# Cached grouped-query attention on one core: how the output weight and two V blocks are spread over the DMA engines, and where two groups of transposes stand

## The chip, the cores and the metric

The kernel runs on one core of a Trainium2 chip. The metric is the device time of one execution in microseconds (us), as a median of runs. A profile of one execution is at hand: its span runs from the first to the last instruction, and the execution's own time is a little longer than that.

## The reference

```python
B, Sq, D = 8, 4, 512
Hq, Hkv, Sk, Dh = 32, 8, 2048, 128          # all tensors bf16
q = (x @ wq).reshape(B, Sq, Hq, Dh).transpose(0, 2, 1, 3)
k = jnp.repeat(k_cache, 4, axis=1)           # k_cache, v_cache: (B, Hkv, Sk, Dh)
v = jnp.repeat(v_cache, 4, axis=1)
scores = jnp.einsum("bhqd,bhkd->bhqk", q, k) * (Dh ** -0.5)
p = softmax(scores, axis=-1)
o = jnp.einsum("bhqk,bhkd->bhqd", p, v)
out = o.transpose(0, 2, 1, 3).reshape(B, Sq, Hq * Dh) @ wo      # wq (512, 4096), wo (4096, 512)
```

The two caches are 32 MB each, wq and wo 4 MB each; everything else is small.

## The kernel before, in words

**Units.** The work is cut into 16 units: a batch entry and a group of four of the eight K/V heads (first all eight entries of one group, then of the other). A unit has one K block and one V block of 2 MB, each laid out as 128 partitions with 16 KB a partition. K0 is the first K block and K15 the last.

**Loads.** All big loads are issued by SP, on one queue. A list fixes their order: K0, wq, x, K1, K2, V0, then K and V in turn. `load_ready` issues what has a free buffer; there are three buffers for K and three for V, so SP waits for the transposes of a K block or the V products of a V block before it issues the load that reuses the buffer. The output weight wo, 4096 rows of 512, is read in four passes p of 1024 rows. Before, passes 0 and 1 come in two shapes: `load_wo_e` brings, in eight small loads strewn between the K and V loads, 64 partitions' worth of rows (eight partitions a load, 64 KB) into the tile `wo_e`; `load_wo_m` brings the remaining 768 rows of a pass into `wo_sb`. Passes 2 and 3 are one load each (`load_wo`). Part of pass 0 goes ahead of V14, the rest of wo after V15. Then come seven loads of 2 to 14 rows of x into the tile `spare`, which nothing reads; they are there to show in a profile when the DMA engines have got so far, and are called probe loads here.

**Step n of the main loop** (n from 1 to 17) works on three units at once. It transposes K of unit n in four parts (`transpose_part`: PE transposes into `kp`, DVE copies to `kt`), makes the scores of unit n - 1 (`scores`: PE matmuls into `s_ps`, ACT exponentials into `s_sb` with row sums), turns the probabilities of unit n - 1 so that the keys lie on partitions (`probs_to_keys`: eight PE transposes into `pt`, four ACT copies into `probs`), and for unit w = n - 2 makes the sums for the normalisation (`norms`), the products with V (`values`, in two halves of 32 matmuls into `o_ps`) and the scaled result `oT` (`finish`). The order in which PE takes these within a step is the order of the source. A manual schedule keeps it; each engine runs its own instructions in order and waits on semaphores.

**Output.** After the eight units of a head group, `to_tokens` turns `oT` to tokens and `to_wo_rows` turns it to the row layout in which wo was loaded (`oE`, `oM` for the first group, `oP` for the second). `project(p, r0, n)` adds n rows of pass p to `out_ps`, two matmuls a row. At the end ACT copies `out_ps` to `out_sb`, and two DMAs, one from ACT and one from SP, write the output.

The lines of the profile that the prediction speaks of are those of the functions above: 97 (K loads), 105 (V loads), 116, 120 and 124 (wo), 400 (probe loads), 177 and 178 (K transposes and copies), 247 and 255 (scores, exponentials), 265 and 271 (`probs_to_keys`), 304 (`values`), 356 (`project`), 409 (the copy to `out_sb`).

Of the kernel before, what the change touches and what calls it, by code (L numbers as in the profile page):

```python
# [8 lines left out]
BF16 = mybir.dt.bfloat16  # L9
# [5 lines left out]
def kernel(  # L15
# [9 lines left out]
    nc = tc.nc  # L25

    B, Sq, D = x.shape
# [4 lines left out]
    T = B * Sq  # L32
    R = D // 128
    G = 4
    S = 128 // G
    C = Sk // S
# [3 lines left out]
    HP = 8  # L40
    WR = 8
    NP = Hq // HP
    DH = D // 2
    NU = (Hkv // G) * B
    KB, VB = 3, 3
    scale = float(Dh) ** -0.5
    AX = mybir.AxisListType.X
    ADD = mybir.AluOpType.add
# [3 lines left out]
    const = ctx.enter_context(tc.tile_pool(name="const", bufs=1))  # L52
# [9 lines left out]
    psum_l = ctx.enter_context(tc.tile_pool(name="psum_l", bufs=1, space=bass.MemoryType.PSUM))  # L62

    order = ctx.enter_context(tc.manual_schedule())

    NE, WE, WM = 64, 4, 6
    assert NE * WE + 128 * WM == HP * 128

    x_sb = const.tile([T, D], BF16, name="x_sb")
    xT_sb = const.tile([128, R, T], BF16, name="xT_sb")
    q_bd = const.tile([128, Hkv // G, 2, G, B, 2, HQ], BF16, name="q_bd")
# [1 line left out]
    ident = const.tile([128, 128], BF16, name="ident")  # L75
# [1 line left out]
    ones = const.tile([128, 128], FP32, name="ones")  # L77
    by_q = const.tile([128, HQ], FP32, name="by_q")
    oT = [const.tile([128, HP, 2, B, Sq], BF16, name=f"oT{n}") for n in range(2)]
    oE = const.tile([NE, WE, 2, T], BF16, name="oE")  # L80
    oM = const.tile([128, WM, 2, T], BF16, name="oM")
    oP = const.tile([128, WR, 2, T], BF16, name="oP")
    nat_sb = const.tile([2 * T, HP * 128], BF16, name="nat_sb")
    out_sb = const.tile([2 * T, DH], BF16, name="out_sb")
    spare = const.tile([16, 8, 32], BF16, name="spare")
    pad = const.tile([128, 32], BF16, name="pad")
    wo_e = const.tile([NE, 2, WE, D], BF16, name="wo_e")
    wq_sb = wpool.tile([128, R, HqDh], BF16, tag="w", name="wq_sb")

    units = [(hq, b) for hq in range(Hkv // G) for b in range(B)]  # L90
# [1 line left out]
    vs = [None] * NU  # L92
# [9 lines left out]
    def load_v(u):  # L102
        hq, b = units[u]
        vs[u] = vpool.tile([128, C, Dh], BF16, tag="v_sb", name="v_sb")
        nc.sync.dma_start(
            vs[u][:, :, :],
            v_cache[b, G * hq : G * hq + G].rearrange("g (s c) d -> (g s) c d", c=C),
        )

    pairs = wo.rearrange("(n p k) j -> n k p j", p=2, k=HP * 128)  # L110

    def load_wo_e(i):

        a = i // 4 * 32 + i % 4
        rows = pairs[0, : NE * WE, :, :].rearrange("(q r) p j -> q p r j", r=WE)
        nc.sync.dma_start(wo_e[a : a + 29 : 4, :, :, :], rows[a : a + 29 : 4, :, :, :])

    def load_wo_m(p):
        rows = pairs[0, NE * WE :, p, :].rearrange("(q r) j -> q r j", r=WM)
        nc.sync.dma_start(wo_sb[:, p, :WM, :], rows)  # L120

    def load_wo(p, r0, n):
        rows = pairs[1, :, p - 2, :].rearrange("(q r) j -> q r j", r=WR)
        nc.sync.dma_start(wo_sb[:, p, r0 : r0 + n, :], rows[:, r0 : r0 + n, :])

    load_k(0)
# [2 lines left out]
    loads = [("k", 1)]  # L129
    for u in range(2, NU + 2):  # L130
        if u < NU:
            loads.append(("k", u))
        if u == NU:
            loads.append(("m", 0))
        loads.append(("v", u - 2))
        if u % 2 == 0 and u < NU:
            loads.append(("e", u // 2 - 1))
    loads.insert(-1, ("e", 7))
    loads.reverse()

    def load_ready(nk, nv):

        while loads:
            kind, u = loads[-1]
            if kind == "m":
                load_wo_m(u)
            elif kind == "e":
                load_wo_e(u)
            elif u >= (nk + KB if kind == "k" else nv + VB):
                return  # L150
            else:
                (load_k if kind == "k" else load_v)(u)
            loads.pop()
# [10 lines left out]
        out=by_q[:, :], in_=ident4[:, :].rearrange("p (c q) -> p q c", q=HQ), axis=AX, op=ADD  # L164
# [4 lines left out]
    def transpose_part(u, t):  # L169

        k4 = ks[u][:, :, :].rearrange("s c d -> s (c d)").bitcast(FP32)
        kt[(u, t)] = ktpool.tile([128, J, 128, 2], BF16, tag="kt", name="kt")
        for half in range(2):
            kp = psum_k.tile([128, J // 2, 128], FP32, tag="k", name="kp")
            for j in range(J // 2):
                w = (t * J + half * J // 2 + j) * 128
                nc.tensor.transpose(kp[:, j, :], k4[:, w : w + 128], ident4[:, :])  # L177
            nc.vector.tensor_copy(  # L178
                out=kt[(u, t)][:, half * J // 2 : (half + 1) * J // 2, :, :].rearrange(
                    "k j s e -> k (j s e)"  # L180
                ),
                in_=kp[:, :, :].rearrange("k j s -> k (j s)").bitcast(BF16),
            )
# [13 lines left out]
    for hq in range(Hkv // G):  # L197
        psq = psum_s.tile([128, rep * Dh], FP32, tag="s", name="psq")
        for r in range(R):
            for g in range(G):  # L200
# [3 lines left out]
                    lhsT=xT_sb[:, r, :],  # L204
                    rhs=wq_sb[:, r, c0 : c0 + rep * Dh],
# [8 lines left out]
    for hq in range(Hkv // G):  # L214
        for e in range(2):
            pse = psum_k.tile([128, rep, G, B, Sq], FP32, tag="k", name="pse")
            for h in range(rep):
                nc.tensor.matmul(
                    pse[:, h, :, :, :].rearrange("d g b s -> d (g b s)"),
                    lhsT=q_nats[hq][:, h, e, :, :].rearrange("t c k -> t (c k)"),  # L220
                    rhs=ident[:, :],
# [3 lines left out]
            for c in range(2):  # L225
                rows = slice(c * 64, (c + 1) * 64)
# [35 lines left out]
    def probs_to_keys(u):  # L262
        pt = psum_t.tile([128, J, 128], BF16, tag="t", name="pt")
        for j in range(J):
            nc.tensor.transpose(  # L265
                pt[:, j, :], s_sbs[u][:, j, :, :].rearrange("q g s -> q (g s)"), ident[:, :]
            )
        pr = probs[u % 2]
        for g in range(G):
            rows = slice(g * S, (g + 1) * S)  # L270
            nc.scalar.copy(  # L271
                out=pr[rows, :, g, :],
                in_=pt[rows, :, :].rearrange("s j (c q) -> s (j c) q", q=HQ),
            )
# [52 lines left out]
        nc.vector.tensor_copy(out=nat_sb[:, :], in_=nat[:, :, :].rearrange("t h d -> t (h d)"))  # L327

    def to_wo_rows(n):
        def turn(cols, parts, w, to):  # L330
            perm = psum_l.tile([parts, w, 2, T], BF16, tag="l", name="perm")
            by_row = nat_sb[:, cols].rearrange("t (q r) -> t r q", r=w)
            for r in range(w):
                nc.tensor.transpose(  # L334
                    perm[:, r, :, :].rearrange("q p t -> q (p t)"),
                    by_row[:, r, :],
                    ident[: 2 * T, : 2 * T],
                )
            nc.vector.tensor_copy(out=to[:, :, :, :], in_=perm[:, :, :, :])

        if n == 0:
            turn(slice(0, NE * WE), NE, WE, oE)
            turn(slice(NE * WE, HP * 128), 128, WM, oM)
        else:
            turn(slice(0, HP * 128), 128, WR, oP)

    def project(p, r0, n):
        for r in range(r0, r0 + n):
            if p >= 2:
                o, w = oP[:, r, p % 2, :], wo_sb[:, p, r]  # L350
            elif r < WE:
                o, w = oE[:, r, p, :], wo_e[:, p, r]
            else:
                o, w = oM[:, r - WE, p, :], wo_sb[:, p, r - WE]
            for half in range(2):
                nc.tensor.matmul(  # L356
                    out_ps[half * T : (half + 1) * T, :],
                    lhsT=o,
                    rhs=w[:, half * DH : (half + 1) * DH],
                    start=(p == 0 and r == 0),  # L360
                    stop=(p == NP - 1 and r == WR - 1),
                )

    for n in range(1, NU + 2):
        w = n - 2
        if n < NU:
            transpose_part(n, 0)
        if n - 1 < NU:
            scores(n - 1)
        if n < NU:  # L370
            transpose_part(n, 1)
        if w >= 0:
            norms(w)
        if n < NU:
            transpose_part(n, 2)
        if n == NU + 1:
            out_ps = psum_s.tile([2 * T, DH], FP32, tag="s", name="out_ps")
            project(0, 0, WE + WM)
            project(1, 0, WE)
        if w >= 0:  # L380
            values(w, 0)
        if n < NU:
            transpose_part(n, 3)
        if n - 1 < NU:
            probs_to_keys(n - 1)
        if w >= 0:
            values(w, 1)
            finish(w)
        if w == B:
            to_tokens(0)  # L390
        if w == B + 1:
            to_wo_rows(0)
        load_ready(min(n + 1, NU), max(w + 1, 0))
        if n == NU - 1:
            assert not loads, loads
            load_wo_m(1)
            for p, r0, k in [(2, 0, 8), (3, 0, 8)]:
                load_wo(p, r0, k)
            for i, k in enumerate([8, 4, 12, 6, 14, 2, 10]):
                nc.sync.dma_start(spare[:k, i, :], x.flatten_outer_dims()[:k, :32])  # L400

    to_tokens(1)
    project(1, WE, WM)
    to_wo_rows(1)
    project(2, 0, WR)
    for r in range(0, WR, 2):
# [35 lines left out]
```

## Time and profile before

| what | value |
|---|---|
| median of 3 runs | 189.48 us (189.43 to 189.7) |
| the profiled execution's own time | 189.72 us |
| its span | 187.9 us |
| granted TensorE clock, mean | 0.955 |
| PE busy | 142.9 us (76%) |
| DVE busy | 104.1 us (55%) |
| ACT busy | 94.6 us (50%) |
| load queue, share of 16 engines' span | 94.8% |
| moved by DMA | 75.91 MB, 404 GB/s over the span |

A line of the page's second section cuts the span into 40 equal slices; each digit is a busy share in tenths. The queue section gives packets, megabytes and the time that they took as a share of 16 engines. In the chain of waits a line has the start in us, the duration in us, and what it was: a piece of work of an engine with its line, a DMA that was waited for, or "issue", where nothing that the profile shows was waited for. PE is TensorE's matmuls, DVE VectorE, ACT ScalarE, SP the engine that issues the loads. The trace also holds a record of each DMA packet (start, duration, bytes) and of each completion count: a load that runs on k DMA engines counts up k times, once as each engine is done.

### The profile page before, as it was taken

The numbers are of one execution on the slowest core, as the hardware profiler recorded it, in microseconds if no ns is written. First come the engines' busy times: TensorE is split into PE (matmuls) and PEld (weight loads), VectorE is DVE, ScalarE is ACT, GpSimd is POOL, SyncE is SP. The second block draws the span as 40 slices with busy tenths as digits, with TensorE's granted clock in tenths as the row PEclk, the third lists the DMA queues.
The fourth block names the chain that finished last, engine by engine and source line by source line (L and its number), as shares of the span: only waits on it lengthen the run. The fifth ranks groups of instructions, "written<-read, shape, count | busy, mean of one in ns | idle before, by whom it ended". The sixth has DMA issues, their size and how long they took to land.

```text
span 187.9 us, 5334 instructions
## 1 busy us (share of the span) xinstructions
PE 142.9 (76%) x2366; PEld 124.7 (66%) x2366; DVE 104.1 (55%) x190; ACT 94.6 (50%) x200; POOL 8.2 (4%) x11
## 2 busy tenths in 40 slices
PE   0192979887979797777777869778777777795883
PEld 0291358786969686667676759577766767695662
DVE  4073285876677767474756656655647474661120
ACT  2000243759394765655647382909274655647800
POOL 8800000000000000000000000000000000000000
PEclk9998556999999999999999999999999999997899
DMA  6998999999999999999999999999999999999930
GB/s 185 485 446 373 429 432 429 425 439 422 427 422 432 434 418 429 439 415 439 425 436 415 436 425 429 429 436 422 429 432 432 425 415 440 416 436 415 400 132 7
DMA packets 5799, 75.91 MB, mean 404 GB/s; under 512 B 816, under 2 KB 912, under 8 KB 1296
## 3 DMA queue, kind: packets, MB, share of 16 engines
q1 hardware_dynamic: 5728, 75.55, 94.8%
q8 instruction: 18, 0.29, 0.6%
q14 instruction: 5, 0.04, 0.1%
q10 hardware_dynamic: 48, 0.02, 0.0%
HBM read 75.53 MB, written 0.03 MB: 402 GB/s over the span
## 4 chain that ended last, share of the span: by engine, by line
DMA 45%; PE 39%; DVE 7%; ACT 5%; issue 1%; SPq 0%; ACTq 0%
DMA k_sb<-in_k_cache_dram 36%; PE kp L177 18%; DMA x_sb<-in_x_dram 9%; PE o_ps L304 8%; DVE kt L178 5%; PE s_ps L247 5%; ACT probs L271 4%; PE psq L202 2%; PE pt L265 2%; PE l_ps L287 2%; PE out_ps L356 1%; DVE by_gq L280 1%; PE perm L334 0%; DVE q_bd L227 0%; PE nat L324 0%
## 5 line engine op out<-in xcount | busy, mean ns | idle before, releaser
L178 DVE COPY kt<-kp 128x1024 bf16<-128x1024 bf16 x128 | 82.2, 683 | 43.5 <-PE kp L177 43.4
L271 ACT COPY probs<-pt 32x1024 bf16<-32x1024 bf16 x64 | 64.2, 1003 | 59.4 <-PE pt L265 58.3
L177 PE MATMUL kp<-ident,k_sb 128*128 128x128 f32 x512 | 72.4, 289 | 17.9 <-DMA k_sb<-in_k_cache_dram 17.5
L177 PEld LDWEIGHTS kp<-ident,k_sb 128*128 128x128 f32 x512 | 60.2, 150 | 23.0 <-issue 14.0
L304 PE MATMUL o_ps<-probs,v_sb 128*128 128x64 bf16 x1024 | 36.1, 195 | 2.7 <-ACT probs L271 1.9
L304 PEld LDWEIGHTS <-v_sb 128*128 128x128 bf16 x1024 | 34.6, 100 | 3.4 <-DMA v_sb<-in_v_cache_dram 2.4
L255 ACT ACTIVATE s_sb<-s_ps 128x256 bf16<-128x256 f32 x64 | 23.7, 384 | 2.1 <-PE s_ps L247 1.7
L287 PE MATMUL l_ps<-by_gq,ones 128*128 128x64 f32 x32 | 6.9, 298 | 15.6 <-DVE by_gq L280 15.6
L247 PE MATMUL s_ps<-kt,q_bd 128*32 128x256 bf16 x512 | 18.8, 288 | 0.0
L287 PEld LDWEIGHTS l_ps<-by_gq,ones 128*128 128x128 f32 x32 | 4.8, 188 | 19.2 <-DVE by_gq L280 17.7
L247 PEld LDWEIGHTS <-q_bd 128*32 128x32 bf16 x512 | 12.7, 97 | 3.8 <-issue 2.7
L295 DVE RECIPROCAL r_sb<-l_ps 128x64 f32<-128x64 f32 x16 | 8.9, 557 | 9.0 <-PE l_ps L287 9.0
L255 ACT ACTIVATION_READ_ACCUMULATOR s_sb<-s_ps 128x1 f32 x64 | 13.2, 206 | 0.0
L314 DVE TENSOR_TENSOR oT<-o_ps,r_sb 128x64 bf16<-128x64 f32 x16 | 3.6, 225 | 16.2 <-PE o_ps L304 16.2
L211 ACT ACTIVATE q_nat<-psq 128x512 bf16<-128x512 f32 x2 | 1.2, 597 | 20.0 <-PE psq L202 20.0
L265 PE MATMUL pt<-ident,s_sb 128*128 128x128 bf16 x128 | 10.2, 225 | 0.0
L265 PEld LDWEIGHTS <-s_sb 128*128 128x128 bf16 x128 | 8.7, 101 | 0.2
L409 ACT CAST out_sb<-out_ps 64x256 bf16<-64x256 f32 x1 | 0.4, 366 | 7.0 <-PE out_ps L356 7.0
L202 PE MATMUL psq<-wq_sb,xT_sb 128*32 128x512 bf16 x32 | 3.6, 631 | 0.3 <-DVE xT_sb L195 0.3
L161 POOL MEMSET probs<- 128x4096 bf16 x1 | 3.5, 3513 | 0.0
L160 POOL MEMSET probs<- 128x4096 bf16 x1 | 3.5, 3512 | 0.0
L280 DVE TENSOR_TENSOR by_gq<-l_sb,by_q 128x64 f32<-128x64 f32 x16 | 3.5, 216 | 0.0
(33 smaller groups left out, 32.2 us busy)
## 6 DMA issues: line engine op xcount, KB each, us to landing
k_sb<-in_k_cache_dram SPq DMA_DIRECT2D x16, 2048.0 KB
v_sb<-in_v_cache_dram SPq DMA_DIRECT2D x16, 2048.0 KB
wq_sb<-in_wq_dram SPq DMA_DIRECT2D x1, 4096.0 KB
wo_sb<-in_wo_dram SPq DMA_DIRECT2D x2, 1024.0 KB
wo_sb<-in_wo_dram SPq DMA_DIRECT2D x2, 768.0 KB
wo_e<-in_wo_dram SPq DMA_DIRECT2D x8, 64.0 KB
x_sb<-in_x_dram SPq DMA_DIRECT2D x1, 32.0 KB
spare<-in_x_dram SPq DMA_DIRECT2D x1, 0.5 KB
```

Source lines behind the costliest of these rows:

```text
L177: nc.tensor.transpose(kp[:, j, :], k4[:, w : w + 128], ident4[:, :])
L178: nc.vector.tensor_copy(out=kt[(u, t)][:, half * J // 2 : (half + 1) * J // 2, :, :].rearrange("k j s e -> k (j s e)"), in_=kp[:, :, :].re ...
L202: nc.tensor.matmul(psq[g * T : (g + 1) * T, :], lhsT=xT_sb[:, r, :], rhs=wq_sb[:, r, c0 : c0 + rep * Dh], start=(r == 0), stop=(r == R - 1),)
L247: nc.tensor.matmul(s_ps[t * 32 : (t + 1) * 32, g % 2, :, :], lhsT=q_bd[:, hq, e, g, b, :, :], rhs=kt[(u, t)][:, :, g * S : (g + 1) * S, e] ...
L255: nc.scalar.activation(out=s_sbs[u][:, :, g, :], in_=s_ps[:, g % 2, :, :], func=EXP, accum_out=l_sbs[u][:, g : g + 1],)
L265: nc.tensor.transpose(pt[:, j, :], s_sbs[u][:, j, :, :].rearrange("q g s -> q (g s)"), ident[:, :])
L271: nc.scalar.copy(out=pr[rows, :, g, :], in_=pt[rows, :, :].rearrange("s j (c q) -> s (j c) q", q=HQ),)
L280: nc.vector.tensor_tensor(out=by_gq[:, :, :], in0=l_sbs[u][:, :].unsqueeze(2).to_broadcast([128, G, HQ]), in1=by_q[:, :].unsqueeze(1).to_b ...
L287: nc.tensor.matmul(l_ps[:, :], lhsT=ones[:, :], rhs=by_gq[:, :, :].rearrange("k g q -> k (g q)"), start=True, stop=True,)
L295: nc.vector.reciprocal(r_sbs[u][:, :], l_ps[:, :])
L304: nc.tensor.matmul(o_pss[u][:, :], lhsT=vs[u][:, 2 * (t * J + j) + c, :], rhs=probs[u % 2][:, i, :, :].rearrange("s g q -> s (g q)"), star ...
L314: nc.vector.tensor_tensor(out=oT[hq][:, :, :, b, :].rearrange("d h p s -> d p h s"), in0=o_pss[u][:, :].rearrange("d (p h s) -> d p h s", ...
```

## The change

It does four things.

- wo is loaded in whole passes of 1024 rows by one function, 128 partitions a load: pass 0 ahead of V14, pass 1, pass 2, and pass 3 in two pieces (six rows a partition and two) after V15. `wo_e`, `oE` and `oM` are gone; the first group's result is turned with eight transposes and one copy into `oP[0]`, where it was ten and two. All of pass 0 is projected ahead of `values(15, 0)`, all of pass 1 in the tail.
- V3 and V9 are loaded in three pieces of 112, 12 and 4 partitions.
- `probs_to_keys(14)` stands ahead of `values(13, 0)`, and `probs_to_keys(15)` ahead of `values(14, 0)`; in the other steps it stays between the halves.
- There are five probe loads, of 1, 3, 5, 9 and 13 rows.

```diff
+    V_CUT = (3, 9)
...
-        nc.sync.dma_start(
-            vs[u][:, :, :],
-            v_cache[b, G * hq : G * hq + G].rearrange("g (s c) d -> (g s) c d", c=C),
-        )
-
-    pairs = wo.rearrange("(n p k) j -> n k p j", p=2, k=HP * 128)
-
-    def load_wo_e(i):
-
-        a = i // 4 * 32 + i % 4
-        rows = pairs[0, : NE * WE, :, :].rearrange("(q r) p j -> q p r j", r=WE)
-        nc.sync.dma_start(wo_e[a : a + 29 : 4, :, :, :], rows[a : a + 29 : 4, :, :, :])
-
-    def load_wo_m(p):
-        rows = pairs[0, NE * WE :, p, :].rearrange("(q r) j -> q r j", r=WM)
-        nc.sync.dma_start(wo_sb[:, p, :WM, :], rows)
+        rows = v_cache[b, G * hq : G * hq + G].rearrange("g (s c) d -> (g s) c d", c=C)
+
+        cuts = (0, 112, 124, 128) if u in V_CUT else (0, 128)
+        for r0, r1 in zip(cuts, cuts[1:]):
+            nc.sync.dma_start(vs[u][r0:r1, :, :], rows[r0:r1, :, :])
 
     def load_wo(p, r0, n):
-        rows = pairs[1, :, p - 2, :].rearrange("(q r) j -> q r j", r=WR)
+        rows = wo[p * HP * 128 : (p + 1) * HP * 128, :].rearrange("(q r) j -> q r j", r=WR)
         nc.sync.dma_start(wo_sb[:, p, r0 : r0 + n, :], rows[:, r0 : r0 + n, :])
...
         if u == NU:
-            loads.append(("m", 0))
+            loads.append(("w", 0))
         loads.append(("v", u - 2))
-        if u % 2 == 0 and u < NU:
-            loads.append(("e", u // 2 - 1))
-    loads.insert(-1, ("e", 7))
...
+        perm = psum_l.tile([128, WR, 2, T], BF16, tag="l", name="perm")
+        by_row = nat_sb[:, :].rearrange("t (q r) -> t r q", r=WR)
+        for r in range(WR):
+            nc.tensor.transpose(
+                perm[:, r, :, :].rearrange("q p t -> q (p t)"), by_row[:, r, :], ident[: 2 * T, : 2 * T]
+            )
+        nc.vector.tensor_copy(out=oP[n][:, :, :, :], in_=perm[:, :, :, :])
...
+        if n == NU - 1:
+            probs_to_keys(n - 1)
         if n == NU + 1:
             out_ps = psum_s.tile([2 * T, DH], FP32, tag="s", name="out_ps")
-            project(0, 0, WE + WM)
-            project(1, 0, WE)
+            project(0, 0, WR)
+        if n == NU:
+            probs_to_keys(n - 1)
         if w >= 0:
             values(w, 0)
         if n < NU:
             transpose_part(n, 3)
-        if n - 1 < NU:
+        if n < NU - 1:
             probs_to_keys(n - 1)
...
-            load_wo_m(1)
-            for p, r0, k in [(2, 0, 8), (3, 0, 8)]:
+            for p, r0, k in [(1, 0, 8), (2, 0, 8), (3, 0, 6), (3, 6, 2)]:
                 load_wo(p, r0, k)
-            for i, k in enumerate([8, 4, 12, 6, 14, 2, 10]):
+            for i, k in enumerate([1, 3, 5, 9, 13]):
                 nc.sync.dma_start(spare[:k, i, :], x.flatten_outer_dims()[:k, :32])
 
     to_tokens(1)
-    project(1, WE, WM)
+    project(1, 0, WR)
```

More of the change, by code (lines that the diff above doesn't have):

```diff
@@ L64 @@
     order = ctx.enter_context(tc.manual_schedule())
-    NE, WE, WM = 64, 4, 6
-    assert NE * WE + 128 * WM == HP * 128
     x_sb = const.tile([T, D], BF16, name="x_sb")
@@ L79 @@
     oT = [const.tile([128, HP, 2, B, Sq], BF16, name=f"oT{n}") for n in range(2)]
-    oE = const.tile([NE, WE, 2, T], BF16, name="oE")
-    oM = const.tile([128, WM, 2, T], BF16, name="oM")
-    oP = const.tile([128, WR, 2, T], BF16, name="oP")
+    oP = [const.tile([128, WR, 2, T], BF16, name=f"oP{n}") for n in range(2)]
     nat_sb = const.tile([2 * T, HP * 128], BF16, name="nat_sb")
     out_sb = const.tile([2 * T, DH], BF16, name="out_sb")
-    spare = const.tile([16, 8, 32], BF16, name="spare")
-    pad = const.tile([128, 32], BF16, name="pad")
-    wo_e = const.tile([NE, 2, WE, D], BF16, name="wo_e")
+    spare = const.tile([16, 5, 32], BF16, name="spare")
     wq_sb = wpool.tile([128, R, HqDh], BF16, tag="w", name="wq_sb")
@@ L144, in load_ready @@
             kind, u = loads[-1]
[L145 to L148, printed above, removed]
+            if kind == "w":
+                load_wo(u, 0, WR)
             elif u >= (nk + KB if kind == "k" else nv + VB):
@@ L329, in to_wo_rows @@
     def to_wo_rows(n):
[L330 to L345, printed above, removed]
+        perm = psum_l.tile([128, WR, 2, T], BF16, tag="l", name="perm")
[5 more added lines that the diff above has]
+        nc.vector.tensor_copy(out=oP[n][:, :, :, :], in_=perm[:, :, :, :])
     def project(p, r0, n):
         for r in range(r0, r0 + n):
[L349 to L354, printed above, removed]
             for half in range(2):
@@ L357, in project @@
                     out_ps[half * T : (half + 1) * T, :],
-                    lhsT=o,
-                    rhs=w[:, half * DH : (half + 1) * DH],
+                    lhsT=oP[p // 2][:, r, p % 2, :],
+                    rhs=wo_sb[:, p, r, half * DH : (half + 1) * DH],
                     start=(p == 0 and r == 0),
```

## The prediction

> **What bounds the kernel now.** I read the page first: busy shares, the 40 slices, the queues. Then the chain of waits in order of time, then the timeline of the last 30 us, and last the packet and completion records of the trace, which tell what each of the 16 DMA engines carried.
>
> ```profile
> span 187.9 us, 5334 instructions
> ...
> DMA  6998999999999999999999999999999999999930
> ...
> q1 hardware_dynamic: 5728, 75.55, 94.8%
> q8 instruction: 18, 0.29, 0.6%
> ```
>
> The load queue keeps all 16 engines busy from 5 us to 180 us; no compute engine is over 76%. So the body is a stream of fixed bytes. The chain of waits shows where it hands over to compute:
>
> ```profile
> 136.83 22.23 DMA k_sb<-in_k_cache_dram
> 159.06 0.14 issue
> 159.19 1.06 PE kp L177 x8
> ...
> 165.67 0.91 PE kp L177 x8
> 166.58 0.46 PE pt L265 x8
> ...
> 167.12 1.01 ACT probs L271
> ...
> 171.26 1.76 PE o_ps L304 x32
> 173.02 0.89 PE pt L265 x8
> ...
> 173.98 1.01 ACT probs L271
> ...
> 178.12 2.04 PE o_ps L304 x64
> 180.16 0.02 issue
> ...
> 183.07 1.94 PE out_ps L356 x32
> 185.01 0.02 issue
> 185.04 0.37 ACT out_sb L409
> ```
>
> The last K block (K15) lands at 159.06. Then ACT rules: four copies of unit 14's probabilities, the exps of unit 15 (171.23 to 172.80 in the timeline), four copies of unit 15's, then V products and the tail to 185.01. SP is not in it: K15 was issued at 136.83, 22 us before it landed, so the queue is deep and the four small loads added on SP (about 0.4 us of issue each) hide under that depth; without it they would cost up to 1.6 us.
>
> **Engines, before.** Each 16 KB packet takes 0.611 us and the next starts after 0.607. A wo_e load puts two 4 KB packets, 0.306 us, on eight engines only. K15's sixteen completions lie between 154.0 and 159.1: the stream is as late as its slowest engine. K15 follows wo_e load 6 in the queue; that load's eight completions (151.2 to 154.2) plus 8 x 0.607 = 4.86 us give the eight wo_e engines in K15: 156.0, 156.1, 156.2, 156.4, 157.7, 158.0, 158.9, 159.1. The other eight are 154.0 to 157.0. The last wo load completes at 177.2, 177.4, nine times from 179.7 to 180.2, then 181.1, 181.4, 181.6, 182.4, 182.6. The probe loads show who is who, since an n-row probe has n completions and the sets nest: latest of the first four engines (A) 181.4, of the next four (B) 182.6, of the third four (C) 180.2, of the last four (D) 181.6. Part of the lag is the 18 instruction packets: the one at 100.50 took 0.968 and stretched the data packet beside it to 1.079, so that engine ended at 102.53 instead of 101.11: 1.42 us late, for good.
>
> **Part 1: no wo_e, two V blocks cut.** Per engine up to K15: A, B lose seven wo_e loads, 7 x 0.306 = 2.14. V3 and V9 in 112 + 12 + 4 rows give each engine 7 rows, A and B and C one more, A another: A +2 rows (+1.21), B and C 0, D -2 rows (-1.21). K15 then completes at latest in A 158.0 - 0.93 = 157.1, B 159.1 - 2.14 = 157.0, C 157.0, D below 157.0. So K15 comes 2.0 us earlier (K14, by the same sum with six loads, 1.7). At the end of the stream all of wo has been loaded in both kernels: before, A and B carried 32 KB over the mean, C and D 32 KB under it; now A +32 KB, B and C 0, D -32 KB. So A 0, B -1.21, C +1.21, D 0: 181.4, 181.4, 181.4, 181.6. The last wo row lands at 181.6 instead of 182.6. V15, before it: A -0.6, B -1.8, C +0.6, D -0.6, so at latest 174.3 instead of 175.8.
>
> No load of 112 rows is in the trace. Bounds: 16 engines with 7 rows each, or, like the 14-row probe, 14 engines with 8. I take 16, since 112 is a multiple of 16 as 128 and x's 32 rows are; 14 is the rival below. The extra loads themselves: between nothing, as the wo_e loads show (DMA share 1.00 from 86 to 96 us, with one in it), and four times the 0.34 us that DMA issue rows take, were it exposed. I take nothing.
> [...]
>
> **Part 2: two probs_to_keys earlier.** Unit 14's transposes (pt, 0.45) now stand ahead of values(13, 0) and transpose_part(15, 3), so they start 0.93 + 0.91 = 1.84 us earlier. Their exps could end at about 161.0 (ACT's copies of unit 13 end 1.7 earlier), pt is reached at about 162.6: no wait. ACT's copies begin at 167.12 - 2.04 - 1.84 = 163.25 and end at 167.3. Delayed by pt: values(13, 0), 0.45, whose V13 lands at 162.0 (163.9 before), and the last transposes of K15; scores(15) keep their place, 167.89 - 2.04 = 165.85. So ACT is free for the exps at 167.3 and finishes them at 168.9 (1.57); before 172.80.
> Unit 15's transposes now stand ahead of both halves of values(14). PE waits there for the exps, and values(14) queues behind it: before, its first half ran under the exps. pt and both halves took 171.26 to 175.30 = 4.04; now 168.95 to 173.0. Norms and the step to project follow as before (0.82), then project(0) with 16 matmuls at 0.76/12 = 0.063: 1.0. PE is at values(15) at 174.85, ACT's copies (173.98 - 3.87 = 170.1, four of 1.01) are done at 174.2, V15 is there at 174.3. So PE sets it, 0.6 after ACT: values(15) starts 3.3 us earlier than 178.12. The waits of probs_to_keys on ACT are on one buffer (pt), free since 167.3.
> The half clock bears on this: PE's granted clock is 0.50 at 173 to 174 (1.00 around), after 1.9 us without PE work. The new gap, 167.3 to 168.95, is 1.6 us. I keep the slow products (1.76 and 1.62 per half); at full speed (0.93) PE would be done 1.9 us earlier and ACT and V15 would set 174.3.
> [...]
>
> **Part 3: the tail.** From the start of values(15) to project(2) it was 183.07 - 178.12 = 4.95; project(1) now does 16 matmuls there instead of 12, +0.25: 174.85 + 5.2 = 180.05, and 1.94 more: PE ends at 182.0. The wo pieces: w1 at 176.7 (needed at 177.8), w2 at 179.2 (needed at 180.05), six rows of w3 at 181.0 (needed at 181.0), the last two at 181.6 (needed at 181.75). Were PE faster, the last two rows would still hold the end at 181.6 + 4 x 0.061 + a little = 181.95. Both roads give 182.0. The merged oP transposes of pass 0 (8 for 10, one copy for two) lie in the middle of the stream and are worth nothing; the other probe loads (0.4 KB) neither.
>
> **Sum.** 185.01 to 182.0 is 3.0 us; with four near ties on the way I take 0.1 off: 2.9. The profiled execution took 189.72 (span 187.9 and 1.8 around it), so it would take 186.8; the median of the runs is 189.48, 0.24 lower: **186.6**.
>
> **Rivals.**
> Instruction packets fall badly (0.20). Eighteen packets at 1.42 us each set the lags, and the 18th came at 179.7, when its engine had nothing left. Compute 3 us earlier brings it to about 176.7, into the stream. In D that makes 180.2 + 1.42 = 181.6, no loss. In C, which has 1.21 more to carry, 182.8: the last wo rows hold PE to 183.1, a gain of 1.9: 187.6. For: turns seem to go round eight engines. Against: the 17th hit D's late engine, and the next in turn was most likely its neighbour.
> The cut is spread otherwise (0.08). With 14 engines of 8 rows, A gets 4 rows more and K15 lands at 158.0 - 2.14 + 2.43 = 158.3, the end at 182.8 (an engine of D that lost nothing): about 187.7. The nested probes speak against it.
> Slower (0.05): the changed program shifts instruction packets onto A, which carries 32 KB extra. Each costs 1.42 after 181.4; two leave 184.2 and still a gain of 0.5, three make 185.7, PE ends at 186.0, 1.0 later: 190.5. It decides from wo's last landing at 184.7. Against: PE loses only 20 instructions, nearly all after the body.
> Faster than forecast (0.07): full clock and all waits hidden, bounded by the last wo rows at 181.2: 186.1.
>
> **Numbers.** The forecast case has 0.60 and its own range 186.1 to 187.2. With the two rivals at 187.6 and 187.7 the range is 186.0 to 187.9, leaving out under 2 in 10. A measurement of this kernel can tell about 0.2% (0.4 us). Faster 0.91, same 0.03 (a mishap of 2.5 us or more that ends near 189.5), slower 0.06.
>
> **What would show it.** Right: the wait for K15 ends near 157.1, unit 14's ACT copies start near 163.3, values(15) near 174.9, the last out_ps matmul ends near 182.0, wo completions end within 1.5 us of each other except for the two untouched engines. Wrong: K15 later than 158.0 (the engine sums fail), unit 14's copies not 3.8 us earlier (part 2 fails), or PE waiting over 0.5 us on wo (a packet fell badly).

## The result, and the profile after

The changed kernel took 201.31 us (median of 4 runs, 200.22 to 202.15), the kernel before 189.45 on the same chip: ratio 1.0625, interval 1.057 to 1.0681. The forecast was 186.6, a gain; it lost 11.9 us. The profiled execution took 202.15 us. (Some executions of every kernel here take 2 to 4 us longer, a few up to 6; the ratios leave out those that could be recognised.)

The page of the kernel after: the span, the two DMA lines of the 40 slices (5.0 us each), the queues.

```profile
span 200.4 us, 5311 instructions
...
DMA  6999999999999899999999999999999999999970
GB/s 203 438 464 402 428 425 432 435 422 425 430 288 227 164 432 428 415 438 425 432 425 432 425 435 321 239 167 376 422 442 428 425 417 442 415 430 424 420 302 12
...
q1 hardware_dynamic: 5662, 75.55, 96.1%
q8 instruction: 18, 0.29, 0.6%
```

The same bytes go through the same queue and the busy digits are 9 almost throughout, as before. The line below them tells the kernels apart: twice, from 55 to 70 us and from 120 to 135 us, the rate falls from some 430 to 164 and 167 GB/s while the engines stay busy. The kernel before has no such dip:

```profile
GB/s 185 485 446 373 429 432 429 425 439 422 427 422 432 434 418 429 439 415 439 425 436 415 436 425 429 429 436 422 429 432 432 425 415 440 416 436 415 400 132 7
```

The transfers between 56 and 70 us, first of the kernel before, then of the kernel after (the DMA view of that window):

```profile
DMA packets 414, 5.99 MB, mean 428 GB/s; under 512 B 48, under 2 KB 48, under 8 KB 48
```
```profile
DMA packets 231, 2.99 MB, mean 214 GB/s; under 512 B 48, under 2 KB 48, under 8 KB 48
```

Half the bytes in the same 14 us, with nothing idle: the packets themselves are longer. A 16 KB packet took 0.611 us before. As the engines come to V3's 112-row piece, from 56.3 us on, the packets lengthen; from 57 to 64 us every one takes 1.05 to 1.3, and once the 12-row piece is under way they go to 1.5 to 1.93 (the longest of the trace, 2.34, is at V9). K6's packets, whole rows as ever, are slow beside them. From 70.3 us on packets take 0.611 to 0.62 again; the last row of V3 lands at 70.9. Summed over the 16 KB packets of the load queue from 20 us on, the excess over 0.611 is 14.87 us per engine, 0.61 in the kernel before.

The chain of waits of the kernel after, in order of time:

```profile
41.49 29.36 DMA v_sb<-in_v_cache_dram
70.99 1.86 PE o_ps L280 x32
...
74.65 20.14 DMA k_sb<-in_k_cache_dram
...
104.52 32.48 DMA v_sb<-in_v_cache_dram
137.14 1.86 PE o_ps L280 x32
...
149.87 21.34 DMA k_sb<-in_k_cache_dram
171.35 1.06 PE kp L153 x8
...
189.76 2.71 PE o_ps L280 x64
195.51 1.94 PE out_ps L317 x32
197.46 0.02 issue
```

V3 and V9, which were in nobody's way before, are now waits of the chain (their last pieces land at 70.9 and 137.0), and K15 lands at 171.2 where 157.1 was forecast: 14.1 us late, close to the 14.3 us by which the excess in the packets grew. From K15's landing to the last matmul it takes 26.23 us, 25.95 before. So K15 is 12.2 us later than before (159.06) and the tail 0.3 longer, together the 12.4 us by which the profiled execution is longer (202.15 for 189.72).

### The profile page after: what moved, and what is told of

Its sections match the earlier page's. It is cut to its first block, busy times and chain, and to the rows that moved or that the text cites. A ratio compares the mean times of both kernels' runs of the same rounds, so it can differ in the third digit from the quotient of the medians.

```text
span 200.4 us, 5311 instructions
## 1 busy us (share of the span) xinstructions
PE 148.1 (74%) x2356; PEld 128.0 (64%) x2356; DVE 103.9 (52%) x189; ACT 94.6 (47%) x200; POOL 8.2 (4%) x11
## 4 chain that ended last, share of the span: by engine, by line
DMA 60%; PE 28%; DVE 4%; ACT 3%; issue 2%; SPq 1%; ACTq 0%
DMA v_sb<-in_v_cache_dram 31%; DMA k_sb<-in_k_cache_dram 21%; PE kp L153 10%; DMA x_sb<-in_x_dram 8%; PE o_ps L280 8%; PE s_ps L223 3%; DVE kt L154 3%; PE out_ps L317 2%; PE psq L178 2%; ACT probs L247 2%; PE pt L241 1%; PE l_ps L263 1%; ACT s_sb L231 1%; SPq L101 1%; PE perm L309 1%
## 5 line engine op out<-in xcount | busy, mean ns | idle before, releaser
L153 PE MATMUL kp<-ident,k_sb 128*128 128x128 f32 x512 | 74.7, 295 | 20.6 <-DMA k_sb<-in_k_cache_dram 20.1
L153 PEld LDWEIGHTS kp<-ident,k_sb 128*128 128x128 f32 x512 | 61.7, 153 | 26.1 <-issue 19.7
L280 PE MATMUL o_ps<-probs,v_sb 128*128 128x64 bf16 x1024 | 38.1, 200 | 5.9 <-DMA v_sb<-in_v_cache_dram 5.7
L280 PEld LDWEIGHTS <-v_sb 128*128 128x128 bf16 x1024 | 36.2, 102 | 7.2 <-issue 6.6
L223 PE MATMUL s_ps<-kt,q_bd 128*32 128x256 bf16 x512 | 19.3, 294 | 0.0
L317 PE MATMUL out_ps<-wo_sb,oP 128*32 128x256 bf16 x64 | 4.9, 310 | 0.5 <-DVE oP L312 0.5
L317 PEld LDWEIGHTS <-oP 128*32 128x32 bf16 x64 | 3.3, 107 | 1.4 <-DVE oP L312 0.6
L136 POOL MEMSET probs<- 128x4096 bf16 x1 | 3.5, 3511 | 0.0
## 6 DMA issues: line engine op xcount, KB each, us to landing
v_sb<-in_v_cache_dram SPq DMA_DIRECT2D x14, 2048.0 KB, 24.5
```

Of the source, the lines that this page charges most:

```text
L223: nc.tensor.matmul(s_ps[t * 32 : (t + 1) * 32, g % 2, :, :], lhsT=q_bd[:, hq, e, g, b, :, :], rhs=kt[(u, t)][:, :, g * S : (g + 1) * S, e] ...
L280: nc.tensor.matmul(o_pss[u][:, :], lhsT=vs[u][:, 2 * (t * J + j) + c, :], rhs=probs[u % 2][:, i, :, :].rearrange("s g q -> s (g q)"), star ...
L317: nc.tensor.matmul(out_ps[half * T : (half + 1) * T, :], lhsT=oP[p // 2][:, r, p % 2, :], rhs=wo_sb[:, p, r, half * DH : (half + 1) * DH], ...
```

## Experiments

**Is it the cut, and are the rest of the sums right?** e1 is the changed kernel with no block cut; e2 is the kernel before with the two blocks cut.

```diff
-    V_CUT = (3, 9)          # e1, from the kernel after
+    V_CUT = ()
```
```diff
-        nc.sync.dma_start(vs[u][:, :, :], ...)          # e2, from the kernel before
+        cuts = (0, 112, 124, 128) if u in (3, 9) else (0, 128)
+        for r0, r1 in zip(cuts, cuts[1:]):
+            nc.sync.dma_start(vs[u][r0:r1, :, :], rows[r0:r1, :, :])
```

> The changed kernel with V3 and V9 loaded whole. Theory A (the cut of the two V blocks carries the whole loss, the rest of the change works as forecast): by the engine sums K15 lands at about 157.0 in the profile, the last wo piece at up to 182.8, and the time is 186.6 to 187.6 us. Theory B (the rest of the change has a cost of its own, for instance PE waiting in the tail): above 189.5 us.

> The kernel before with only V3 and V9 cut into 112, 12 and 4 rows. Theory A: two stretches of some 14 us with about half the DMA rate, each costing about 6 us, so 200 to 203 us. Theory B: clearly less than 200 us, the remainder belonging to the other edits.

e1 took 189.81 us (median of 10), ratio 0.9966 (0.9928 to 1.0004). e2 took 205.31 and 210.3 in two runs, over its range of 200 to 203, against some 189.5; 425 packets after the first 20 us take over 0.64 us, 20 in the kernel before. The cut alone costs all that was lost and more; without it the rest of the change gains a little at most, and by e1 alone that is not clear of noise. e12 is e1 once more, with runs of its own:

> The uncut kernel again, beside the two others of this call: 189.0 to 189.8 us, by its first runs.

189.3 us (median of 12), ratio 0.9953 (0.9926 to 0.9979). Both are over theory A's 186.6 to 187.6: the rest of the change brings less than was forecast. The timeline of e1 (start, duration, engine, line, operation; in brackets the idle time before it and what ended it) gives the forecast's landmarks:

```profile
157.27 1.06 PE L153 MATMUL kp<-ident,k_sb 128*128 128x128 f32 x8 [0.94 <-DMA k_sb<-in_k_cache_dram]
...
163.36 4.05 ACT L247 COPY probs<-pt 32x1024 bf16<-32x1024 bf16 x4 [2.19 <-PE pt L241]
...
169.05 0.62 PE L241 MATMUL pt<-ident,s_sb 128*128 128x128 bf16 x8 [1.53 <-ACT s_sb L231]
...
169.76 4.09 ACT L247 COPY probs<-pt 32x1024 bf16<-32x1024 bf16 x4 [0.77 <-PE pt L241]
...
175.46 3.60 PE L280 MATMUL o_ps<-probs,v_sb 128*128 128x64 bf16 x64 [2.06 <-DMA v_sb<-in_v_cache_dram]
...
183.03 1.92 PE L317 MATMUL out_ps<-wo_sb,oP 128*32 128x256 bf16 x32 [0.52 <-DVE oP L312]
```

K15's last completion is at 157.1; the transposes, copies and exponentials of units 14 and 15 stand where the working put them (163.25, 168.95, 170.1). Then the last V products wait for V15, and take 3.60 us instead of 2.04; the last 32 matmuls of project, from 183.03, end at 184.97, where the kernel before ended at 185.01.

**Is it the number of rows or the place?** e3 cuts V3 and V9 of the kernel before into rows 0 to 63 and 64 to 127. e4 cuts them in the kernel after into strided pieces, spread over all partitions.

```diff
+        cuts = (0, 64, 128) if u in (3, 9) else (0, 128)          # e3
```
```diff
-        cuts = (0, 112, 124, 128) if u in V_CUT else (0, 128)     # e4
+        cuts = ((0, 127, 2), (1, 126, 4), (3, 124, 8), (7, 96, 8), (103, 128, 8))
+        for r0, r1, step in cuts if u in V_CUT else whole:
+            nc.sync.dma_start(vs[u][r0:r1:step, :, :], rows[r0:r1:step, :, :])
```

> The kernel before with V3 and V9 loaded as two halves of 64 neighbouring rows. Theory A1 (place: in a whole load each engine has its own eight neighbouring rows, and pieces of neighbouring rows bring several engines onto one place, in SBUF or in memory): two engines share each place of eight rows, a block takes about 9.7 us where it took 4.9, so 196 to 200 us, with 16 KB packets near 1.2 us. Theory A2 (row counts that are not powers of two, or loads on fewer than 16 engines, are slow whatever their place): no change, 189 to 190 us, packets at 0.611 us.

> The changed kernel with the same 7 + 1 + 1 packets for each engine, but in strided pieces of 64, 32, 16, 12 and 4 rows, so that almost every engine stays on the eight rows that it has in a whole load. Theory A1 (place): no slow packets, and the time that was forecast, 186 to 188 us. Theory A2 (loads on 12 and on 4 engines are slow): still above 193 us.

e3: 208.0 us (two runs), ratio 1.095 (1.0733 to 1.1167), packets mostly of 1.1 to 1.8 us, though each half runs on 16 engines. The packets are those of A1; the time is 8 us over its range. Its transfers from 55 to 70 us:

```profile
DMA packets 244, 3.29 MB, mean 219 GB/s; under 512 B 43, under 2 KB 43, under 8 KB 43
```

e4: 191.63 us, ratio 1.0109 (1.0069 to 1.0149). Its 64-row and 32-row pieces ran at 0.611; slow packets (mostly 0.9 to 1.2 us) came only with the pieces 8 partitions apart, some 2 us a block. Neither of the times expected of it came true: place matters, and "spread out" is not yet the rule.

**Which side, memory or SBUF?** e5 takes the two apart. V3: neighbouring partitions from every other row of the memory. V9: every other partition from neighbouring rows.

```diff
+        if u == 3: parts = [(lower, even), (upper, odd)]      # e5; (to, of); lower = 0..63, even = 0::2
+        if u == 9: parts = [(even, lower), (odd, upper)]
+        for to, of in parts:
+            nc.sync.dma_start(vs[u][to, :, :], rows[of, :, :])
```

> The kernel before, with V3 and V9 each in two loads of 64 rows. V3 goes to neighbouring partitions (0 to 63, 64 to 127) from alternating rows of memory; V9 goes to alternating partitions from neighbouring rows of memory. So the keys of these two blocks stand in another order than the probabilities assume, and the output differs from the reference there. Theory SBUF (several engines on one group of eight partitions slow each other): V3 slow, with 16 KB packets of 1.2 to 1.8 us near 57 to 72 us, V9 clean; about 197 to 199 us. Theory memory (several engines in one 128 KB stretch of memory slow each other): V3 clean, V9 slow near 122 to 137 us; about 197 to 199 us. If either side suffices, both are slow and the time is near 207 us.

199.23 us (one run). Its transfers from 56 to 72 us (V3) and from 122 to 137 us (V9):

```profile
DMA packets 259, 3.47 MB, mean 217 GB/s; under 512 B 47, under 2 KB 47, under 8 KB 47
...
DMA packets 464, 6.50 MB, mean 433 GB/s; under 512 B 66, under 2 KB 66, under 8 KB 68
```

V3 is slow and V9 is not. With e3 (neighbours on both sides, slow) and e4's 64-row piece (strided on both, clean) all four cases are there: only the SBUF side decides.

**Why are pieces 8 partitions apart slow?** e6 varies the small pieces of e4; e9 brings V9 as eight pieces of 16 rows, 8 apart, so that each engine has one packet a piece, and V3 in strides of 2 and 4.

```diff
+        if u == 3: cuts = ((0, 127, 2), (1, 126, 4), (3, 124, 8), (7, 128, 8))            # e6
+        if u == 9: cuts = ((0, 127, 2), (1, 126, 4), (3, 124, 8), (7, 64, 8), (71, 128, 8))
```
```diff
+        if u == 3: cuts = ((0, 127, 2), (1, 126, 4), (3, 128, 4))                         # e9
+        if u == 9: cuts = tuple((r, 121 + r, 8) for r in range(8))
```

> The changed kernel with V3 in strided pieces of 64, 32, 16 and 16 rows (always 16 engines, each on its own eight rows) and V9 in strided pieces of 64, 32, 16, 8 and 8 rows (the last two on eight engines; the first eight rows are those that these engines have in a whole load, the other eight are those of the other engines). Theory place, with chunk i of a load on engine i: V3 clean at 0.611 us a packet; V9 clean until the last piece and slow there, about 2 us lost. Theory few engines (a load on fewer than 16 engines slows the others): V3 clean, V9 slow from the first piece of eight on. Theory small pieces: V3 slow as well from its pieces of 16 rows on. The time is 188 to 191 us in all cases; the packets decide.

> The changed kernel with V3 in strided pieces of 64, 32 and 32 rows and V9 in eight strided pieces of 16 rows; always 16 engines, each on its own eight partitions. Theory single packet (a load that gives an engine one 16 KB packet slows all engines, even on its own partitions; pieces with two or four packets do not): V3 clean, V9 slow from its first piece on, some 3 to 5 us lost. Rival (what was left in the strided runs came from something else than the number of packets): V9 clean as well, and about 189 to 190 us.

e6 took 193.24 us, over its range, and both blocks were slow, V3 without any piece of fewer than 16 engines. e9 took 196.52; V9 lost some 7 us, more than the 3 to 5 expected. Its transfers from 56 to 72 us (V3) and from 115 to 120 us, where V9's first pieces go:

```profile
DMA packets 507, 6.81 MB, mean 425 GB/s; under 512 B 91, under 2 KB 91, under 8 KB 91
...
DMA packets 104, 0.98 MB, mean 197 GB/s; under 512 B 44, under 2 KB 44, under 8 KB 44
```

Strides of 2 and 4 are clean, a stride of 8 is slow from its first piece on. Two readings were left: one packet an engine is slow as such, or partitions 8 apart have something in common. e13 tells them apart, and e14 asks whether a cut costs anything by itself.

```diff
+        if u == 3: cuts = ((32, 96, 1), (0, 29, 4), (1, 30, 4), (2, 31, 4), (3, 32, 4), (96, 128, 1))      # e13
+        if u == 9: cuts = ((32, 93, 4), (33, 94, 4), (34, 95, 4), (35, 96, 4), (0, 32, 1), (96, 128, 1))
```
```diff
+        cuts = ((0, 127, 2), (1, 128, 2)) if u in V_CUT else ((0, 128, 1),)                                # e14
```

> [...] V3 comes as partitions 32-95, then 0-31 in four pieces of 8 partitions 4 apart, then 96-127; V9 as 32-95 in four pieces of 16 partitions 4 apart, then 0-31, then 96-127. [...] Theory Q (one packet an engine is slow by itself, and neighbours too): V9 is slow from its first 16-row piece on, as in the run with eight pieces 8 apart. Theory R (an engine must keep to its own eight neighbouring partitions): both blocks are slow from their first piece on, packets of 1.1 us or more; 199 us or more.

> V3 and V9 in two pieces each, the even and the odd partitions. [...] If a cut costs by its number of loads, or if partitions an engine does not write in a whole load are slow, the two blocks show packets over 0.64 us and the time is 190.5 us or more.

e13's transfers from 57 to 58.5 us (V3's 64 neighbours, 32 to 95), from 119.2 to 121.4 us (V9's four 16-row pieces 4 apart, on the engines that were done with K9), and from 122 to 130 us (0-31 and 96-127 among them):

```profile
DMA packets 46, 0.67 MB, mean 448 GB/s; under 512 B 5, under 2 KB 5, under 8 KB 5
...
DMA packets 85, 0.98 MB, mean 447 GB/s; under 512 B 25, under 2 KB 25, under 8 KB 25
...
DMA packets 168, 1.67 MB, mean 209 GB/s; under 512 B 66, under 2 KB 66, under 8 KB 66
```

K9's earliest engine is done at 119.1 and four packets of 0.607 later, at 121.5, with its share of the four pieces. Up to 121.3 every packet takes 0.611; the slow ones begin as the first engines come to partitions 0 to 31. So sixteen rows with one packet an engine are clean 4 apart (447 GB/s) and slow 8 apart (197 in e9), and 64 neighbours are clean at 32 to 95 (448) and slow at 0 to 63 (in e5's cut into 0 to 63 and 64 to 127 the rate is 217): Q and R fall, and what decides is which set of partitions a piece reaches. What the slow sets have in common, no run shows. The time was 198.57 us (one run).

e14 has no packet longer than before beside the two blocks; from 58 to 72 us, with both halves of V3:

```profile
DMA packets 431, 6.00 MB, mean 429 GB/s; under 512 B 64, under 2 KB 64, under 8 KB 64
```

Its time was 191.01 us, ratio 0.9984 (0.9925 to 1.0042), with runs from 188.65 to 191.81: over the uncut kernel's 189.3 (e12) and over the 190.5 expected of a cut that costs, but without the packets over 0.64 us at the two blocks that were expected with it; its profile shows packets of 0.68 us from 18 to 50 us, far from the blocks. Two loads for one cost nothing that can be seen in their packets; the time alone could not tell.

**What is left of the gain?** e10 is e1 with `probs_to_keys` in its old place; e7 is e1 with pass 0 of wo loaded after V15 and projected behind the last V products; e8 is e1 with 32 idle matmuls ahead of the last V products, to keep the clock up; e11 is e7 with 24 of them.

```diff
-        if n == NU - 1: probs_to_keys(n - 1)     # e10: both early calls out, the old one back for all n
-        if n == NU:     probs_to_keys(n - 1)
```
```diff
-        if u == NU: loads.append(("w", 0))       # e7: the load of pass 0 behind V15
+    loads.append(("w", 0))
-            project(0, 0, WR)                    # and its project behind values(15, 1)
```
```diff
+            for j in range(32):                  # e8; e11 with 24 on top of e7
+                nc.tensor.matmul(fill[:, j % 4, :], lhsT=ident[:, :], rhs=ident[:, :], start=True, stop=True)
```

> The changed kernel uncut and with probs_to_keys between the halves of values in every step, as before; wo still in whole passes. Theory: in the uncut kernel V15's landing (175.4) takes up most of what the earlier transposes bring, since ACT's last copies would end at about 176.0 without them; 0.2 to 0.9 us slower than the uncut kernel, 189.3 to 190.3 us. Rival: the earlier transposes bring their full 1.8 us or more: 191 us and above.

> The changed kernel uncut, with pass 0 of wo loaded after V15 instead of before V14, and project(0) after the V products of the last unit. Theory: in the uncut kernel V15 (landing at 175.4) and not ACT held the tail; 64 KB less ahead of it on each engine bring it to about 173.0, ACT's copies (173.9) become the last wait, and the end moves to the last wo rows at about 183.1: 187.3 to 188.5 us. Rival: PE still falls to half clock in the pause before it (about 1.5 us without work) and the gain over the uncut kernel is under 0.5 us.

> The changed kernel uncut, with 32 matmuls of the identity into an unused PSUM tile ahead of the V products of the last unit, so that PE works while it waits for V15. Theory clock: the pause before V15 (2.1 us) sets the half clock that made the 64 products take 3.6 us instead of 2.0 and the steps behind them about 0.9 us longer; with PE at work they run at full clock and the end moves from 185.0 to the last wo rows at about 183.4: 187.5 to 188.5 us. Rival: the clock falls in any case, or the filler delays the products: no gain over the uncut kernel (189 to 190 us).

> The uncut kernel with pass 0 of wo after V15, project(0) after the last V products, and 24 matmuls of the identity ahead of these products. Theory: with V15 out of the way and the clock kept up, the last wo rows alone set the end (about 183.1 in the uncut profile, plus 0.3): 187.8 to 188.4 us. Rival: 188.6 us or more, as with either edit alone, since these rows set the end there already.

| kernel | median, us | ratio to before | interval |
|---|---|---|---|
| e12 (uncut) | 189.3 | 0.9953 | 0.9926 to 0.9979 |
| e10 (old order) | 189.43 | 0.9962 | 0.9934 to 0.9989 |
| e8 (filled) | 188.98 | 0.9954 | 0.9917 to 0.9992 |
| e7 (wo last) | 188.77 | 0.9937 | 0.9907 to 0.9967 |
| e11 (e7, filled) | 189.48 | 0.9981 | 0.9936 to 1.0026 |

e10 does not differ from e12: part 2, worth 3.8 us at unit 14's copies, is worth nothing that shows at the end. e8 and e11 show no gain over e12 either. e7 has the lowest ratio and is faster than the kernel before, but its interval overlaps that of e12. e7, e8 and e11 all missed the ranges of their theories.

The profiles of these four have packets of 0.68 us between 18 and 58 us, so K15 lands 2.8 us later than in e12 (3.6 in e7). Counted from K15's landing their tails can be compared. Here are the last V products of e10, then those of e8 and its last 16 matmuls:

```profile
179.11 2.03 PE L280 MATMUL o_ps<-probs,v_sb 128*128 128x64 bf16 x64 [1.11 <-ACT probs L247]
...
178.34 2.04 PE L280 MATMUL o_ps<-probs,v_sb 128*128 128x64 bf16 x64 [0.29 <-DMA v_sb<-in_v_cache_dram]
...
185.03 1.05 PE L317 MATMUL out_ps<-wo_sb,oP 128*32 128x256 bf16 x16 [0.53 <-DMA wo_sb<-in_wo_dram]
```

In e8 the products take 2.04 us, as they did in the kernel before at a granted clock of 1.00 (178 to 180 us), and 2.79 in e12, so the idle matmuls do their work; but then the last 16 matmuls wait for wo, and the last ends 26.2 us after K15, 26.9 in e12. In e7 and e11, too, the last 16 matmuls wait for wo: the last rows of wo hold the end, and that is why these edits bring so little. In e10 ACT starts the products 19.2 us after K15 for 18.6 in e12, but they take 2.03 us for 2.79, and the end comes at 26.4. By these two profiles the old order loses 0.6 us at the start of the products and gets it back at their clock, after a pause of 1.1 us instead of 2.3.

## Why the prediction was wrong

**The step that failed** is "The extra loads themselves: between nothing, as the wo_e loads show [...], and four times the 0.34 us that DMA issue rows take, were it exposed. I take nothing." Both ends of that bound were wrong in kind. They price a load by its issue and its count of bytes; the cost lay in the time of each packet, mostly 1.05 to 1.9 us and up to 2.34 instead of 0.611, for all 16 engines and for K6 beside it. The measured term is about 7 us a block (K6 lands at 75.4, in e1 at 68.3), 14.1 at K15. The row it was read from was near in size and far in what counted: a wo_e load puts 4 KB packets on eight engines, to partitions 4 apart.

**What the runs show of the cause.** Two loads for one show no price of their own: V3 in even and odd rows runs at 429 GB/s (e14), the whole block at 428. What decides is the set of partitions that a piece reaches. The rate is halved with 0 to 63 and 64 to 127 (217 GB/s in e5, 219 in e3), with sixteen rows 8 apart (197 in e9) and with the stretches 0 to 31 and 96 to 127 (209 in e13); it is kept with 32 to 95 (448, and 447 in rows 4 apart, e13) and with every other partition (433 in e5, 429 in e14). Why these sets differ is not shown. Nor is it shown why the packets are longest (1.5 to 1.93 us at V3) once the 12 rows 112 to 123 are under way, or why the 112-row piece alone has 1.05 to 1.3 us on all engines: how its rows are dealt to the engines was not tried apart. That piece is more than half of the 7 us a block (an estimate: seven packets an engine, each some 0.55 us longer), so for the larger part of the loss the cut is shown as the cause, and the way it works is not.

**The engine sums were right.** "K15 at 157.1" was met to 0.1 us in e1 and e12 (without the cut the sum gives 157.0), and so were unit 14's copies (163.36 for 163.25) and unit 15's transposes (169.05 for 168.95). Counted from K15's landing, the sums with the cut hold in the changed kernel too: V15 lands 17.45 us after K15 (17.2 forecast), the last wo row 24.8 (24.5). That K15 later than 158.0 would mean "the engine sums fail" was a wrong reading fixed in advance: the bytes were counted rightly, the packet time was taken as a constant. The cut was not needed for K15: its sixteen completions spread 3.1 us in e1 and 3.2 with the cut, 5.1 before. At the end of the stream it did what it was meant to do: the last wo load's completions spread 3.6 us after, 4.8 in e12 and 5.4 before.

**Of the 2.9 us, 1.03 came uncut in e12's profile, next to nothing in e1's.** In e12 the last matmul ends at 183.98, in e1 at 184.97 (before 185.01, forecast 182.0). The last V products of e12 start at 175.63 for 174.85, 0.8 late, because V15 lands late on one engine: fifteen are done by 174.1, the last at 175.6 (an instruction packet that began at 170.1 and took 0.97 us fits the lag, by inference). "V15 at latest 174.3" holds only with the cut, which relieves the engines called D; without it the prediction's own terms give 175.5 for them (174.9 before, and 0.6 more). In the same way they give 182.8 for the last wo row (181.6 and 1.2 more), and it came at 182.9. The other 1.2 us are the clock. The windows of e12 (PE, PEld, DVE, ACT, POOL busy with counts, then the granted clock, the DMA share, GB/s):

```profile
173.00:175.00 2.00, 0.31 (x6) 0.03 (x2) 0.00 (x0) 0.76 (x1) 0.00 (x0) 1.00 0.98 414
175.00:177.00 2.00, 1.37 (x41) 1.37 (x42) 0.00 (x0) 0.00 (x0) 0.00 (x0) 0.91 1.01 425
177.00:179.00 2.00, 1.68 (x30) 1.52 (x28) 0.23 (x1) 0.00 (x0) 0.00 (x0) 0.50 0.81 332
```

PE stands 2.3 us for V15 and then has half the clock: the 64 products take 2.79 for 2.04, the eight transposes of nat 1.06 for 0.63. At full clock the last wo rows would still have held the end at about 183.15 (an estimate: 182.9 and four matmuls of 0.061).

**The clock term was in the wrong place.** The prediction kept the products of unit 14 slow (1.76 and 1.62) and took those of unit 15 as fast. In e12 unit 14's 64 products took 2.03 at full clock, PE was ready for unit 15 at 173.3, and the half clock came there. In the changed kernel both were slow, 3.04 and 2.71, and the project between them took 1.89 for 1.0; the granted clock is 0.50 from 186 to 190 us. So its last matmul comes 26.2 us after K15's landing where the forecast had 24.9: a second miss, of 1.3 us. This also fits what e10 shows of part 2: it brings PE and ACT earlier to a block that is not there, and after the longer pause (2.3 us in e12, 1.1 in e10) the products take 2.79 us for 2.03.

**The rivals.** None gave the outcome. The 182.8 of the rival with the instruction packets is near the 182.9 of e12, but the engines D give the same figure without the cut, so e12 does not speak for it. The one slower rival (packets onto engines 0 to 3, 190.5) has no sign in the trace: the queue of instruction packets has 18, as before. The one that should have stood there is "a cut block slows the stream", with its place at V3 and V9.

## What to carry to other kernels

A load's cost is not its bytes over the rate: here two pieces of 64 neighbouring partitions, 0 to 63 and 64 to 127, halved the rate of everything in flight (217 for 428 GB/s, e5), and 112 neighbouring rows did so too (224 in the changed kernel from 57 to 64 us). Of the cuts tried, only every other partition (e14, 429 GB/s) and strides of 2 and 4 (e9, 425) left the packets as they were. Rows 32 to 95 were clean by themselves (448, e13), but they leave 0 to 31 and 96 to 127, which were slow (209). A cut that evens out the engines and keeps the packets at 0.611 was not found. To see it, read the GB/s line against the DMA busy line: here busy at 9 with the rate halved (167 GB/s, packets up to 2.34 us) was long packets, not missing ones. And when a wait is moved away, look for the landings just behind it (here V15 and the last rows of wo) before counting the gain.

## What was not expected of the hardware

The slow-down is shared: while V3's last pieces land, packets of another load to its usual partitions are slow as well (the changed kernel's K6, 1.5 to 1.9 us), and it ends within a packet of V3's last row (70.3 to 70.9 us). A pause of 2.1 us (e1) and 2.3 us (e12) in TensorE's work was followed by half the clock for some 7 and 3 us, and the 64 products behind it took 3.60 and 2.79 us; with 32 matmuls in the pause (e8) they took 2.04. The length of the pause alone does not decide: ahead of unit 15's transposes, 1.52 us was followed by half the clock in the changed kernel (0.50 from 185 to 191 us, the 64 products took 3.04) and 1.53 us was not in e1 (2.03).
